# A pair that always runs is moved behind the branches of pairs, one key load to another queue, and the first expert output to another bank

## The chip, the cores and the metric

The kernel runs on one core of a Trainium2 chip. The metric is the device time of the execution in microseconds (us). The profile is one execution taken by the hardware profiler. Engines are named as it names them: PE is TensorE's matmuls, PEld its weight loads, DVE is VectorE, ACT ScalarE, POOL GpSimd, SP SyncE; a q behind a name (POOLq) is the engine's instruction queue.

## The reference

Sparse attention over 8 batches, 8 heads, 576 positions and 64 columns a head, half of the heads with a local mask and half with a strided one. Its output, 4608 rows of 512, goes into a mixture of 8 experts. Each row has one expert, chosen at run time:

```python
for s in range(S):
    fresh_e = int(np.argmax(logits[b, s]))
    if s == 0 or local_gate[b, s] < 0.5:
        e = fresh_e
    else:
        e = prev_e if prev_e >= 0 else fresh_e
    prev_e = e
    ...                                       # p: softmax of the logits
    h = np.maximum(x[b, s] @ w1[e], 0.0)      # 512 -> 1024
    out[b, s] = p[e] * (h @ w2[e])            # 1024 -> 512
```

Which rows an expert gets, and so how many tiles of 128 rows there are, is known only on the chip.

## The kernel before

Attention runs first and writes its rows to a buffer in DRAM (`xd`). Six expert tiles of early batches ("early" tiles) begin under its end. Then the router's counts are known, and the rest follows as a list of units `U`: *pairs* (two tiles of one expert, done with a Strassen-like scheme of seven products a layer), two *mixed* tiles (two halves of different experts) and *singles*. For a unit the kernel loads the expert's weights (`weights`, 4 MB in four pieces), gathers the rows (`gather`, an indirect DMA from GpSimd), turns them with transposes (`turn_x`, done one unit ahead, in the middle of the unit before), computes the hidden layer and the output, and scatters the result.

The numbers of the plan: eleven pairs are certain (`PAIR_MIN` is 11), up to sixteen may be needed (`PAIR_MAX`), and up to four singles.

```python
for k in range(PAIR_MIN):
    self.U.append(pair(k))
    ...                                        # a mixed tile after pairs 2 and 5
self.first = len(self.U)
self.U += [dict(rd=r2, ..., single=i) for i in range(SINGLES)]
self.last = len(self.U)
self.U += [pair(k) for k in range(PAIR_MIN, PAIR_MAX)]
for j, u in enumerate(self.U):
    u["set"] = j % 2 if j < self.last else 2 if j == self.last else (j - self.last - 1) % 2
...
for j, u in enumerate(self.U):
    ahead = self.first if j == self.last else j
    at = j - AHEAD if j < NE else self.first - 1 if j == self.last + 1 else ahead - 2
    self.gathers.setdefault(at, []).append(j)
    if j > 1:
        self.turns.setdefault(ahead - 1, []).append(j)
```

A unit turns the rows of the next one between its own hidden layer and its own output. For a pair, VectorE then builds the sums of rows (`xs`, four adds) and of weights (`t1`, four adds) that the seven products need:

```python
def unit(self, j, loads, nxt, step=lambda ins: None):
    ...
    self.hidden_pair(j)                 # sums of w2 (t2), then seven products
    ...
    for k in nxt:
        self.turn_x(k)
    self.output_pair(j)                 # seven products, two scatters
```

In the hidden layer the products of one bank form a chain, and ScalarE copies it out between them; VectorE's adds and ScalarE's relus stand in the same queues:

```python
product(chain, a11, b11, True);   nc.scalar.copy(out=p, in_=chain)
product(b7, s3, t3, True)
product(chain, s2, t2, False);    nc.scalar.copy(out=u, in_=chain)
product(b2, a12, b21, True);      row(b2, p, flat[0])     # row: VectorE add, ScalarE relu
nc.vector.tensor_tensor(u, b7, u, op=Alu.add)
product(chain, s1, t1, False);    nc.scalar.copy(out=v, in_=chain)
row(b7, v, flat[3])
product(b4, a22, t4, True);       row(b4, u, flat[2])
product(chain, s4, b22, False);   nc.scalar.activation(flat[1], chain, Act.Relu)
self.rows = self.sums_a(self.hs, hs)
```

The branches. All engines read the counts into registers and compare; where a branch is not taken, each engine jumps and adds to its semaphores what the branch would have added:

```python
for j in range(NE - 1, self.first):
    self.run(j)
singles, pairs = count(1, SINGLES), count(0, PAIR_MAX)
with ExitStack() as chain:
    for j in range(self.first, self.last):
        chain.enter_context(tc.If(singles > j - self.first))
        self.run(j)
for j in range(self.last, len(self.U)):
    ctx.enter_context(tc.If(pairs > self.U[j]["pair"]))      # closed at line 252
    self.run(j)
```

Behind all this the kernel asks whether the softmax without subtracted maximum was safe, and skips a careful second pass of everything if so:

```python
again = nc.values_load(bad[0:1, 0:1], ...)     # line 143
with tc.If(again > 0):                         # line 145
    ...
    passes(tc, True, ...)
```

Of the kernel before, what the change touches and what calls it, by code (L numbers as in the profile page):

```python
# [19 lines left out]
P = 128  # L20
# [251 lines left out]
def attention(ctx, tc, careful, psX, psS, fill, q, k, vl, vs, wg, xd, cc, codes, inv):  # L272
# [113 lines left out]
    def load_first():  # L386


        for n in range(2 * PAIRS + 2):
            if n == PAIRS + 2:  # L390
                nc.sync.dma_start(out=wgs[:, :, GC // 2:], in_=wg.rearrange("(k p) e -> p k e", p=P))
            if n < 2 * PAIRS:
                b, pair = divmod(n, PAIRS)
                grp, i2 = divmod(pair, 2)
                if i2 == 0:
                    places(b, grp)
                qt, kt = st["q", b, grp], st["k", b, grp]
                hq, hk = LT // 2 * LQ, LT // 2 * LQ + STRIDE
                for c, d in (((slice(0, hq), slice(0, hk)), (slice(hq, S), slice(hk, KW))) if n == 0 else
                             ((slice(0, S), slice(0, KW)),)):  # L400
                    nc.sync.dma_start(out=qt[:, i2, c], in_=q[b][:, pair, c])
                    (nc.sync if n else nc.scalar).dma_start(out=kt[:, i2, d], in_=k[b][:, pair, d])
            if n >= 2:
                b, pair = divmod(n - 2, PAIRS)
                grp, i2 = divmod(pair, 2)
                nc.sync.dma_start(out=st["v", b, grp][:, i2], in_=(vs if grp else vl)[b][:, i2])
# [478 lines left out]
class Experts:  # L885
# [14 lines left out]
    def __init__(self, ctx, tc, xd, w1, w2, views, c, r1, r2):  # L900
        self.tc, self.nc = tc, tc.nc
        self.xd, self.w1, self.w2, self.views, self.c = xd, w1, w2, views, c
        self.r1, self.r2 = r1, r2
        xp = ctx.enter_context(tc.tile_pool(name="xp", bufs=1))
        self.end = self.rows = None
        self.sets = [(xp.tile([P, DK, F], F32, name=f"w1t{i}"), xp.tile([P, FK, D], F32, name=f"w2t{i}"))
                     for i in range(1)]
        self.xg = Ring(xp, AHEAD + 1, [P, DX], "xg")
        self.xT = Ring(xp, 2, [P, D], "xgT")
        self.hT = Ring(xp, 2, [P, FK, P], "hT")  # L910
        self.pe = Ring(xp, 2, [P, 2, E], "pe")
        self.pt = Ring(xp, 2, [P, 2], "pt")
        self.pt2 = Ring(xp, 2, [P, 2], "pt2")

        self.U = [dict(rd=r1, at=i, cols=[i], rows=BE * S) for i in range(NE)]
        pair = lambda k: dict(rd=r2, at=k, cols=[2 * k, 2 * k + 1], rows=N, pair=k)
        for k in range(PAIR_MIN):
            self.U.append(pair(k))  # L920
            if k in MIXED:
                m = MIXED.index(k)
                self.U.append(dict(rd=r2, at=PAIR_MAX + SINGLES + m, cols=[2 * PAIR_MAX + SINGLES + m], rows=N,
                                   halves=[r2.units + 2 + 2 * m + h for h in range(2)]))
        self.first = len(self.U)
        self.U += [dict(rd=r2, at=PAIR_MAX + i, cols=[2 * PAIR_MAX + i], rows=N, single=i) for i in range(SINGLES)]
        self.last = len(self.U)
        self.U += [pair(k) for k in range(PAIR_MIN, PAIR_MAX)]
        for j, u in enumerate(self.U):
            u["set"] = j % 2 if j < self.last else 2 if j == self.last else (j - self.last - 1) % 2  # L930
        ones = [u for u in self.U if "pair" not in u]
        for i, u in enumerate(ones):
            u["xg"], u["xT"], u["hT"] = self.xg[i], self.xT[i], self.hT[i]

        self.gathers, self.turns, self.extra = {}, {}, {}
        for j, u in enumerate(self.U):
            ahead = self.first if j == self.last else j
            at = j - AHEAD if j < NE else self.first - 1 if j == self.last + 1 else ahead - 2  # L940
            self.gathers.setdefault(at, []).append(j)
            if j > 1:
                self.turns.setdefault(ahead - 1, []).append(j)
            if "halves" in u or j == self.last:
                w = self.weights(j, int(j != self.last))
                self.extra[ahead - 3], self.extra[ahead - 2] = w[:2], w[2:]

    def later(self, ctx):

        self.banks = Banks(ctx.enter_context(self.tc.tile_pool(name="pse", bufs=1, space=PSUM)))  # L950
        self.banks.ring.used = 3
# [24 lines left out]

    def gather(self, j):
        u = self.U[j]
        if "pair" in u:
            u["xg"] = self.xg2.next()  # L980
        for a, i in enumerate(u["cols"]):
            self.nc.gpsimd.indirect_dma_start(  # L982
                out=u["xg"][:, a] if "pair" in u else u["xg"], out_offset=None, in_=self.xd[0:u["rows"]],
                in_offset=bass.IndirectOffsetOnAxis(ap=u["rd"].gi[:, i:i + 1], axis=0))

    def turn_x(self, j):

        nc, u = self.nc, self.U[j]
        n = len(u["cols"])
        x = u["xg"] if "pair" in u else u["xg"].rearrange("p (a d) -> p a d", a=1)  # L990
        to = self.xT2 if "pair" in u else u["xT"].rearrange("p (a d) -> p a d", a=1)
        for a in range(n):
            ps = self.bank()
            for kk in range(DK):
                self.product(nc.tensor.transpose, ps[:, kk * P:(kk + 1) * P], x[:, a, kk * P:(kk + 1) * P],
                             self.c.ident)
            if "pair" in u:
                nc.scalar.copy(out=to[:, a], in_=ps)
            else:
                ins = nc.vector.tensor_copy(to[:, a], ps).ins  # L1000

        pe, u["pt"] = self.pe.next(), (self.pt2 if "pair" in u else self.pt).next()
        with self.tc.issue_after(ins if n == 1 else self.rows) if n == 1 or self.rows else nullcontext():
            nc.vector.tensor_tensor(pe[:, 0:n], x[:, :, D:DX], across(u["rd"].oh[:, u["at"]], [P, n, E]), op=Alu.mult)
            self.turned = nc.vector.tensor_reduce(u["pt"][:, 0:n], pe[:, 0:n], axis=AX.X, op=Alu.add).ins
            if "pair" in u:
                self.sums_a(self.xs, self.blocks_x())
                self.sums_b(self.t1, self.blocks_w(self.sets[u["set"]][0]))

    def sums_a(self, s, blocks):  # L1010
        v, (a11, a12, a21, a22) = self.nc.vector, blocks
        v.tensor_tensor(s[:, 0], a21, a22, op=Alu.add)
        v.tensor_tensor(s[:, 1], s[:, 0], a11, op=Alu.subtract)
        v.tensor_tensor(s[:, 2], a11, a21, op=Alu.subtract)
        return v.tensor_tensor(s[:, 3], a12, s[:, 1], op=Alu.subtract).ins

    def sums_b(self, t, blocks):

        v, (b11, b12, b21, b22) = self.nc.vector, blocks
        v.tensor_tensor(t[:, 0], b12, b11, op=Alu.subtract)  # L1020
        v.tensor_tensor(b12, b22, b12, op=Alu.subtract)  # L1021
        v.tensor_tensor(t[:, 1], b22, t[:, 0], op=Alu.subtract)
        v.tensor_tensor(t[:, 2], b21, t[:, 1], op=Alu.subtract)  # L1023

    def blocks_x(self):
        x = self.xT2.rearrange("p a (k m) -> p a k m", k=DK)
        return [x[:, a, k:k + DK // 2] for a in range(2) for k in (0, DK // 2)]

    def blocks_w(self, w):
        k, f = w.shape[1] // 2, w.shape[2] // 2  # L1030
# [10 lines left out]

    def hidden_pair(self, j):
        nc = self.nc
        w1, w2 = self.sets[self.U[j]["set"]]
        self.sums_b(self.t2, self.blocks_w(w2))
        a11, a12, a21, a22 = self.blocks_x()
        b11, t3, b21, b22 = self.blocks_w(w1)
        s1, s2, s3, s4 = (self.xs[:, i] for i in range(4))
        t1, t2, t4 = (self.t1[:, i] for i in range(3))
# [29 lines left out]
        row(b4, u, flat[2])  # L1079
        product(chain, s4, b22, False)  # L1080
        nc.scalar.activation(flat[1], chain, Act.Relu)
        self.rows = self.sums_a(self.hs, hs)

    def output_pair(self, j):

# [40 lines left out]

    def hidden_mixed(self, j):

        nc, xT = self.nc, self.U[j]["xT"]
        for f in range(2):  # L1130
            ps = self.bank()
            for kk in range(DK):
# [20 lines left out]
    def hidden_blocks(self, j, pool=None):  # L1153

        nc, u = self.nc, self.U[j]
        w1, xT, hT = self.sets[u["set"]][0], u["xT"], u["hT"]
# [68 lines left out]
    def run(self, j, step=lambda ins: None):  # L1225
# [2 lines left out]
            self.gather(k)  # L1228


        if self.last <= j < len(self.U) - 1:
            for piece in self.weights(j + 1):
                piece()
        loads = self.weights(j + 2) if j + 2 < self.last else []
        for i, piece in enumerate(self.extra.get(j, [])):
# [21 lines left out]
    def rest(self, ctx):  # L1257
# [77 lines left out]
```

## Time and profile before

| | |
|---|---|
| device time, median of 3 | 679.09 us (678.66 to 679.68) |
| span of the profiled execution | 674.9 us |
| mean granted TensorE clock | 0.988 of full speed |
| HBM read, written | 159.80 MB, 19.55 MB |
| last matmul ends | 656.4 us |

The span runs from the first to the last instruction of the profile and lies a few us under the device time. A slice of the page is a fortieth of the span, 16.9 us. Where a helper records all operations (line 1039 for the products, line 371 for VectorE in attention), operations are told apart by their tiles. The profiler counts branches, semaphores, register loads and drains as not busy; the view of a single line shows them with their times.

### The profile page before, as it was taken

The page shows a single profiled execution, that of the slowest core. Times are in us where ns is not written, and L with a number is a line of the kernel's source. Part 1 is how long each engine was busy: PE and PEld are TensorE (multiplying, and loading weights), DVE is VectorE, ACT ScalarE, POOL GpSimd, SP SyncE. Part 2 cuts the span into 40 slices and gives each one's busy share as a digit, 9 for nine tenths or more (in the row PEclk, how much of TensorE's full clock was granted, in tenths as well). Part 3 has the DMA queues.
Part 4 walks back from the last instruction along what each step waited for, and adds up shares of the span by engine and source line. Part 5 has one row for each costly group of instructions (what it writes and reads, how often), then busy time and mean ns, then how long its engine had stood idle before and what let it go on. Part 6 is the DMA issues. An engine that isn't in the chain of part 4 may idle for free.

```text
span 674.9 us, 14639 instructions
## 1 busy us (share of the span) xinstructions
PE 652.1 (97%) x5926; PEld 554.1 (82%) x5926; DVE 392.7 (58%) x805; ACT 188.7 (28%) x390; POOL 156.3 (23%) x200
## 2 busy tenths in 40 slices
PE   9999999999999999999999999999999999999990
PEld 8898888777767799996699984999999996869970
DVE  8686889634561556856295673569569530205660
ACT  4555545421111231322123221322322311113220
POOL 2444444540034311201121102112112011011210
PEclk9999999999999999999999999999999999999995
DMA  9999999559989988776868858675687758577200
GB/s 327 400 408 411 329 326 337 152 157 401 401 290 295 389 303 307 267 281 209 299 223 300 301 189 290 212 241 165 240 300 257 281 178 333 200 268 294 65 18 21
DMA packets 70849, 179.94 MB, mean 267 GB/s; under 512 B 12110, under 2 KB 12622, under 8 KB 70768
## 3 DMA queue, kind: packets, MB, share of 16 engines
q1 hardware_dynamic: 58704, 148.47, 61.1%
q0 software_dynamic: 11776, 30.08, 13.5%
q8 instruction: 51, 0.84, 0.5%
q10 hardware_dynamic: 288, 0.31, 0.1%
q14 instruction: 30, 0.25, 0.1%
HBM read 159.80 MB, written 19.55 MB: 266 GB/s over the span
## 4 chain that ended last, share of the span: by engine, by line
PE 90%; DVE 4%; DMA 2%; issue 1%; ACT 0%; POOL 0%; DVEq 0%; POOLq 0%; ACTq 0%
PE bank L1039 49%; PE bank L1188 10%; PE bank L1162 10%; PE vps L366 6%; PE xps L366 5%; PE sps L366 5%; PE bank L1184 2%; DMA w2t<-in_w_dram 2%; PE sps L1162 1%; DVE e L371 1%; DVE xl L371 0%; DVE lane L841 0%; DVE xs L371 0%; DVE t L1023 0%; DVE w2t L1021 0%
## 5 line engine op out<-in xcount | busy, mean ns | idle before, releaser
L1198 POOL DMA_INDIRECT out_dram<-y,si x38 | 49.4, 1300 | 278.0 <-DVE y L1107 147.0
L982 POOL DMA_INDIRECT xg<-xd,gi x42 | 47.5, 1131 | 146.3 <-PE bank L1039 128.6
L1188 PE MATMUL bank<-w2t,hT 128*128 128x512 f32 x160 | 70.9, 594 | 0.8 <-ACT hT L1165 0.8
L1162 PEld LDWEIGHTS bank<-xgT,w1t 128*128 128x128 f32 x576 | 65.4, 192 | 2.0 <-issue 1.7
L1162 PE MATMUL bank<-xgT,w1t 128*128 128x128 f32 x576 | 66.2, 276 | 0.0
L1188 PEld LDWEIGHTS bank<-w2t,hT 128*128 128x128 f32 x160 | 29.5, 190 | 34.5 <-issue 32.5
L495 POOL DMA_DIRECT2D xd<-xs x80 | 44.9, 567 | 48.1 <-DVE gsm L575 17.3
L1074 DVE TENSOR_TENSOR part<-bank,part 128x512 f32<-128x512 f32 x13 | 9.0, 692 | 78.8 <-ACT part L1071 78.8
L1039 PEld LDWEIGHTS bank<-xT,w1t 128*128 128x128 f32 x416 | 49.5, 192 | 3.1 <-issue 2.6
L1039 PE MATMUL bank<-xT,w1t 128*128 128x128 f32 x416 | 51.3, 276 | 0.0
L1039 PE MATMUL bank<-xs,w1t 128*128 128x128 f32 x416 | 50.7, 275 | 0.0
L1039 PE MATMUL bank<-xs,t 128*128 128x128 f32 x416 | 50.7, 275 | 0.0
L1039 PE MATMUL bank<-w2t,h 128*128 128x256 f32 x208 | 49.2, 379 | 0.0
L1039 PE MATMUL bank<-w2t,hs 128*128 128x256 f32 x208 | 49.1, 379 | 0.0
L1039 PE MATMUL bank<-t,hs 128*128 128x256 f32 x208 | 49.1, 379 | 0.0
L1039 PEld LDWEIGHTS bank<-xs,w1t 128*128 128x128 f32 x416 | 48.5, 192 | 0.0
L1039 PEld LDWEIGHTS bank<-xs,t 128*128 128x128 f32 x416 | 48.5, 192 | 0.0
L1064 DVE TENSOR_TENSOR h<-bank,part 128x512 f32<-128x512 f32 x39 | 27.0, 692 | 34.7 <-ACT part L1076 22.9
L366 PE MATMUL sps<-qt,kt 64*128 64x96 f32 (+2 forms) x704 | 46.3, 277 | 0.2
L366 PEld LDWEIGHTS sps<-qt,kt 64*128 64x128 f32 (+2 forms) x704 | 40.6, 184 | 5.1 <-issue 2.6
L423 ACT ACTIVATE e<-sps 128x576 f32<-128x576 f32 (+1 forms) x64 | 39.9, 649 | 15.7 <-PE sps L366 12.4
L1104 ACT ACTIVATE part<-bank,pt 128x256 f32<-128x256 f32 x39 | 18.5, 474 | 92.0 <-PE bank L1039 92.0
(271 smaller groups left out, 1039.7 us busy)
## 6 DMA issues: line engine op xcount, KB each, us to landing
w1t<-in_w_dram SPq DMA_DIRECT2D x56, 1024.0 KB
w2t<-in_w_dram SPq DMA_DIRECT2D x56, 1024.0 KB
kt<-in_k_dram SPq DMA_DIRECT2D x12, 608.0 KB
qt<-in_q_dram SPq DMA_DIRECT2D x12, 576.0 KB
vlt<-in_vl_dram SPq DMA_DIRECT2D x6, 780.0 KB
xd<-xl POOLq DMA_DIRECT2D x16, 288.0 KB
vst<-in_vs_dram SPq DMA_DIRECT2D x6, 650.0 KB
xd<-xs POOLq DMA_DIRECT2D x48, 54.0 KB
```

The costliest lines, as they stand in the source:

```text
L366: st["pe"] = product(*args, **kw).ins
L423: nc.scalar.activation(ev, ps[0:kb, :, 0:m * w], Act.Exp, bias=0.0, scale=1.0 / DH ** 0.5)
L495: nc.gpsimd.dma_start(out=dst[h, :, c:c + n], in_=src[h * HALF:h * HALF + n * SP // 2, t])
L982: self.nc.gpsimd.indirect_dma_start(out=u["xg"][:, a] if "pair" in u else u["xg"], out_offset=None, in_=self.xd[0:u["rows"]], in_offset=ba ...
L1039: self.end = fn(*args, **kw).ins
L1064: nc.vector.tensor_tensor(to, ps, add, op=Alu.add)
L1074: nc.vector.tensor_tensor(u, b7, u, op=Alu.add)
L1104: nc.scalar.activation(to, ps, Act.Copy, scale=g[r])
L1162: ins = nc.tensor.matmul(ps[:, i * P:(i + 1) * P], lhsT=w1[:, kk, c], rhs=xT[:, kk * P:(kk + 1) * P], start=(kk == 0), stop=(kk == DK - 1))
L1184: ins = nc.tensor.matmul(ps[s], lhsT=hT[:, kk, s], rhs=w[:, kk, :], start=(kk == 0), stop=(kk == FK - 1))
L1188: ins = nc.tensor.matmul(ps, lhsT=hT[:, kk], rhs=w2[:, kk, :], start=(kk == 0), stop=(kk == FK - 1))
L1198: self.nc.gpsimd.indirect_dma_start(out=self.views[0], in_=y, in_offset=None, bounds_check=N - 1, oob_is_err=False, out_offset=bass.Indire ...
```

## The change

It has three parts, and some rewriting that they need.

*The order of the pairs.* Pairs 9 and 10, both certain, leave the place ahead of the singles. Pair 9 stands directly behind the singles, without a branch. Pairs 11 to 15 follow in their nested branches. Pair 10 comes last, behind all branches. The aim is that the work which skipping a branch needs lies ahead of a pair's arithmetic and not at the end of the program. Since the pair before the last one is not known until run time, the last pair's rows are gathered and turned in pair 9 already, its weights are loaded there into the third buffer set, and its turned rows and sums lie in tiles of the singles that are free by then (`xg`, `xT`, `hT`, `y`, `h`).

*Keys of the second pair of heads.* Their load is issued from ScalarE's queue, no longer from SyncE's behind the others.

*The first output's bank.* The ring of eight PSUM banks starts at 6, not at 3.

The rewriting: rows and sums are lists of views in place of one tile, and the product of gate weights with the one-hot choice is one VectorE instruction a tile, not one a pair.

```diff
@@ load_first
-                    (nc.sync if n else nc.scalar).dma_start(out=kt[:, i2, d], in_=k[b][:, pair, d])
+                    (nc.sync if n > 1 else nc.scalar).dma_start(out=kt[:, i2, d], in_=k[b][:, pair, d])
@@ the list of units
-        for k in range(PAIR_MIN):
+        for k in range(PAIR_MIN - 2):
...
-        self.U += [pair(k) for k in range(PAIR_MIN, PAIR_MAX)]
+        self.U += [pair(k) for k in (PAIR_MIN - 2, *range(PAIR_MIN, PAIR_MAX), PAIR_MIN - 1)]
+        self.end_j = len(self.U) - 1
         for j, u in enumerate(self.U):
-            u["set"] = j % 2 if j < self.last else 2 if j == self.last else (j - self.last - 1) % 2
+            u["set"] = j % 2 if j < self.last else 1 if j == self.end_j else (2, 0)[(j - self.last) % 2]
...
-            ahead = self.first if j == self.last else j
-            at = j - AHEAD if j < NE else self.first - 1 if j == self.last + 1 else ahead - 2
+            ahead = self.first if j == self.last else self.last + 1 if j == self.end_j else j
+            at = self.last if j == self.end_j else j - AHEAD if j < NE else self.first - 1 if j == self.last + 1 else ahead - 2
@@ later
-        self.banks.ring.used = 3
+        self.banks.ring.used = 6
@@ gather
+        if j == self.end_j:
+            u["xg"] = [self.xg[a] for a in range(2)]
+            u["xT"] = [self.xT[a] for a in range(2)]
+            u["xs"] = [self.y[i // 2].rearrange("p (i k m) -> p i k m", i=2, m=P)[:, i % 2] for i in range(4)]
+            u["t1"] = [t.rearrange("p (k f) -> p k f", k=DK // 2) for t in
+                       [self.hT[i].rearrange("p k m -> p (k m)") for i in range(2)] + [self.h]]
@@ turn_x
-            nc.vector.tensor_tensor(pe[:, 0:n], x[:, :, D:DX], across(u["rd"].oh[:, u["at"]], [P, n, E]), op=Alu.mult)
+            for a in range(n):
+                nc.vector.tensor_tensor(pe[:, a], x[a][:, D:DX], u["rd"].oh[:, u["at"]], op=Alu.mult)
@@ run
-        if self.last <= j < len(self.U) - 1:
-            for piece in self.weights(j + 1):
+        if self.last <= j < self.end_j - 1:
+            pieces = self.weights(j + 1)
+            if j == self.last:
+                w = self.weights(self.end_j)
+                pieces = pieces[:2] + w[:2] + pieces[2:] + w[2:]
+            for piece in pieces:
                 piece()
@@ rest
-        for j in range(self.last, len(self.U)):
-            ctx.enter_context(tc.If(pairs > self.U[j]["pair"]))
-            self.run(j)
+        self.run(self.last)
+        with ExitStack() as chain:
+            for j in range(self.last + 1, self.end_j):
+                chain.enter_context(tc.If(pairs > self.U[j]["pair"]))
+                self.run(j)
+        self.run(self.end_j)
```

More of the change, by code (lines that the diff above doesn't have):

```diff
@@ L978, in gather @@
         u = self.U[j]
-        if "pair" in u:
-            u["xg"] = self.xg2.next()
+        if j == self.end_j:
[4 more added lines that the diff above has]
+                       [self.hT[i].rearrange("p k m -> p (k m)") for i in range(2)] + [self.h]]
+        elif "pair" in u:
+            x = self.xg2.next()
+            u["xg"], u["xT"] = [x[:, a] for a in range(2)], [self.xT2[:, a] for a in range(2)]
+        else:
+            u["xg"], u["xT"] = [u["xg"]], [u["xT"]]
         for a, i in enumerate(u["cols"]):
             self.nc.gpsimd.indirect_dma_start(
-                out=u["xg"][:, a] if "pair" in u else u["xg"], out_offset=None, in_=self.xd[0:u["rows"]],
+                out=u["xg"][a], out_offset=None, in_=self.xd[0:u["rows"]],
                 in_offset=bass.IndirectOffsetOnAxis(ap=u["rd"].gi[:, i:i + 1], axis=0))
@@ L988, in turn_x @@
         nc, u = self.nc, self.U[j]
-        n = len(u["cols"])
-        x = u["xg"] if "pair" in u else u["xg"].rearrange("p (a d) -> p a d", a=1)
-        to = self.xT2 if "pair" in u else u["xT"].rearrange("p (a d) -> p a d", a=1)
+        n, x, to = len(u["cols"]), u["xg"], u["xT"]
         for a in range(n):
@@ L994, in turn_x @@
             for kk in range(DK):
-                self.product(nc.tensor.transpose, ps[:, kk * P:(kk + 1) * P], x[:, a, kk * P:(kk + 1) * P],
+                self.product(nc.tensor.transpose, ps[:, kk * P:(kk + 1) * P], x[a][:, kk * P:(kk + 1) * P],
                              self.c.ident)
             if "pair" in u:
-                nc.scalar.copy(out=to[:, a], in_=ps)
+                nc.scalar.copy(out=to[a], in_=ps)
             else:
-                ins = nc.vector.tensor_copy(to[:, a], ps).ins
@@ L1002, in turn_x @@
-        pe, u["pt"] = self.pe.next(), (self.pt2 if "pair" in u else self.pt).next()
+                ins = nc.vector.tensor_copy(to[a], ps).ins
+        pe, u["pt"] = self.pe.next(), (self.pt2 if "pair" in u and j != self.end_j else self.pt).next()
         with self.tc.issue_after(ins if n == 1 else self.rows) if n == 1 or self.rows else nullcontext():
-            nc.vector.tensor_tensor(pe[:, 0:n], x[:, :, D:DX], across(u["rd"].oh[:, u["at"]], [P, n, E]), op=Alu.mult)
+            for a in range(n):
+                nc.vector.tensor_tensor(pe[:, a], x[a][:, D:DX], u["rd"].oh[:, u["at"]], op=Alu.mult)
@@ L1005, in turn_x @@
             self.turned = nc.vector.tensor_reduce(u["pt"][:, 0:n], pe[:, 0:n], axis=AX.X, op=Alu.add).ins
             if "pair" in u:
-                self.sums_a(self.xs, self.blocks_x())
-                self.sums_b(self.t1, self.blocks_w(self.sets[u["set"]][0]))
+                if j != self.end_j:
+                    u["xs"], u["t1"] = [self.xs[:, i] for i in range(4)], [self.t1[:, i] for i in range(3)]
+                self.sums_a(u["xs"], self.blocks_x(u))
+                self.sums_b(u["t1"], self.blocks_w(self.sets[u["set"]][0]))
@@ L1010, in sums_a @@
     def sums_a(self, s, blocks):
         v, (a11, a12, a21, a22) = self.nc.vector, blocks
[L1012 to L1015, printed above, removed]
+        v.tensor_tensor(s[0], a21, a22, op=Alu.add)
+        v.tensor_tensor(s[1], s[0], a11, op=Alu.subtract)
+        v.tensor_tensor(s[2], a11, a21, op=Alu.subtract)
@@ L1017, in sums_b @@
+        return v.tensor_tensor(s[3], a12, s[1], op=Alu.subtract).ins
     def sums_b(self, t, blocks):
         v, (b11, b12, b21, b22) = self.nc.vector, blocks
-        v.tensor_tensor(t[:, 0], b12, b11, op=Alu.subtract)
+        v.tensor_tensor(t[0], b12, b11, op=Alu.subtract)
         v.tensor_tensor(b12, b22, b12, op=Alu.subtract)
[L1022 to L1027, printed above, removed]
+        v.tensor_tensor(t[1], b22, t[0], op=Alu.subtract)
@@ L1029, in blocks_w, with blocks_x @@
+        v.tensor_tensor(t[2], b21, t[1], op=Alu.subtract)
+    def blocks_x(self, u):
+        x = [t.rearrange("p (k m) -> p k m", k=DK) for t in u["xT"]]
+        return [x[a][:, k:k + DK // 2] for a in range(2) for k in (0, DK // 2)]
     def blocks_w(self, w):
@@ L1043, in hidden_pair @@
         nc = self.nc
-        w1, w2 = self.sets[self.U[j]["set"]]
-        self.sums_b(self.t2, self.blocks_w(w2))
-        a11, a12, a21, a22 = self.blocks_x()
+        u = self.U[j]
+        w1, w2 = self.sets[u["set"]]
+        self.sums_b([self.t2[:, i] for i in range(3)], self.blocks_w(w2))
+        a11, a12, a21, a22 = self.blocks_x(u)
         b11, t3, b21, b22 = self.blocks_w(w1)
-        s1, s2, s3, s4 = (self.xs[:, i] for i in range(4))
-        t1, t2, t4 = (self.t1[:, i] for i in range(3))
+        (s1, s2, s3, s4), (t1, t2, t4) = u["xs"], u["t1"]
         h11, h12, h21, h22 = hs = [self.h2[:, i] for i in range(4)]
@@ L1081, in hidden_pair @@
         nc.scalar.activation(flat[1], chain, Act.Relu)
-        self.rows = self.sums_a(self.hs, hs)
+        self.rows = self.sums_a([self.hs[:, i] for i in range(4)], hs)
     def output_pair(self, j):
@@ L1127, in hidden_mixed @@
     def hidden_mixed(self, j):
-        nc, xT = self.nc, self.U[j]["xT"]
+        nc, xT = self.nc, self.U[j]["xT"][0]
         for f in range(2):
@@ L1155, in hidden_blocks @@
         nc, u = self.nc, self.U[j]
-        w1, xT, hT = self.sets[u["set"]][0], u["xT"], u["hT"]
+        w1, xT, hT = self.sets[u["set"]][0], u["xT"][0], u["hT"]
         for g in range(FK // self.HB):
```

## The prediction

> **What bounds the kernel now.** I read first the page's busy shares and slices, then the end of the timeline, then the views of single lines that hold branches, semaphores and register loads, which the page leaves out of its busy time. First the page of the kernel before, shares and slices:
>
> ```profile
> PE 652.1 (97%) x5926; PEld 554.1 (82%) x5926; DVE 392.7 (58%) x805; ACT 188.7 (28%) x390; POOL 156.3 (23%) x200
> ...
> PE   9999999999999999999999999999999999999990
> DMA  9999999559989988776868858675687758577200
> ```
>
> TensorE is busy in every slice but the last, and DMA is saturated only in the first seven. So a change pays only if it takes TensorE work away, closes a TensorE gap, or shortens that last slice. I listed every gap of over 0.15 us between matmul records: they sum to 4.0 us, 1.5 of it ahead of the first matmul. The rest of what is not TensorE is the tail. The timeline of the end (start, duration, engine, line; two stretches of one view):
>
> ```profile
> 643.26 1.04 PE L1039 MATMUL bank<-ident,xg 128*128 128x128 f32 x8
> 643.52 0.60 ACT L1081 ACTIVATE h<-bank 128x512 f32<-128x512 f32 x1 [0.49 <-PE bank L1039]
> ...
> 644.13 1.89 PE L1039 MATMUL bank<-w2t,h 128*128 128x256 f32 x8
> ...
> 656.47 0.47 ACT L1104 ACTIVATE y<-bank,pt 128x256 f32<-128x256 f32 x1 [2.97 <-PE bank L1039]
> 657.22 1.01 POOL L1198 DMA_INDIRECT out_dram<-y,si  x1 [1.91 <-ACTq L252]
> ```
>
> The last matmul ends at 656.38, the last scatter starts at 657.22, and the span is 674.88: 17.66 us follow the last scatter with no arithmetic in them. What they are, by lines: L252 closes the branches of pairs, L143 and L145 ask whether the careful second pass is needed, L1331 ends the program (columns: engine's queue, operation, count, shortest/median/longest ns, first and last start). Of L252:
>
> ```profile
> L252 PEldq COMPARE_BRANCH  x4: 71/125/3709, 598.2 to 657.6; - x4
> ...
> L252 POOLq EVENT_SEMAPHORE  x4: 17/43/3462, 657.2 to 660.8; - x4
> ...
> L252 ACTq EVENT_SEMAPHORE  x1: 17/17/17, 657.0 to 657.0; - x1
> L252 PEldq EVENT_SEMAPHORE  x1: 51/51/51, 657.3 to 657.3; - x1
> L252 POOLq INC_SWDGE_SEM  x1: 1646/1646/1646, 660.9 to 660.9; - x1
> ```
>
> Of L143, then L145, then L1331:
>
> ```profile
> L143 POOLq TENSOR_LOAD <-bad x1: 300/300/300, 662.8 to 662.8; - x1
> ```
>
> ```profile
> L145 POOLq EVENT_SEMAPHORE  x6: 17/30/43, 665.8 to 666.3; - x6
> ...
> L145 POOLq COMPARE_BRANCH  x1: 50/50/50, 663.1 to 663.1; - x1
> L145 POOLq INC_SWDGE_SEM  x1: 1628/1628/1628, 666.3 to 666.3; - x1
> ```
>
> ```profile
> L1331 POOLq DRAIN  x3: 46/107/6032, 668.0 to 674.6; - x3
> ```
>
> The reader sees GpSimd alone carrying the tail, one step after another: it waits 3.46 us for the last scatter to land (657.23 to 660.69), makes up the counts of the branches not taken (1.65), loads the flag, jumps (663.1 to 665.8, 2.7 us until its next instruction), makes up the counts of the pass not taken (1.63), drains (6.03), and closes (0.85). The other engines are through with theirs by 663.
>
> **What the Trainium skill says.** Runtime: NRT & Kernel Launch, section Instruction fetch mechanics: a taken branch to a target outside the loaded pages waits for a fetch. The trace agrees: of TensorE's four L252 branches the one that jumps takes 3709 ns, the shortest 71. DMA: Bandwidth & Descriptors, Anatomy of one DMA — SWDGE (gpsimd) path: a transfer's semaphore fires only when the write is confirmed, about 2 us of fixed cost; the scatter here takes 3.46, which I use. The same page, Issuing engines are not separate DMA queues: another issuing queue saves issue time, not bandwidth; no run here shows it yet. Advanced Engine Details and Errata, Engine Queue Depths: TensorE's queue holds many instructions. The trace agrees: that branch was issued at 653.57, 2.8 us before the last matmul ended.
>
> **The change part by part.** Thirteen pairs ran (L1074 x13) and all four singles (L1188 x160 is ten outputs of 16 records, six of them early). So pairs 11 and 12 are taken, 13 is not. Before, the untaken branch comes after all work. After, the order is pairs 0 to 8, singles, 9, 11, 12, the untaken branch, and pair 10 last.
>
> 1. *Tail.* The L252 bookkeeping (landing wait, 1.65 us of counts, branch) moves to the join ahead of pair 10, where GpSimd has some 20 us until it is needed. Behind the last scatter remain the flag, the jump, one count, the drain. Flag and jump take 0.4 + 2.7 = 3.1 us and now run while the scatter lands (3.5 us). New tail from the scatter: 3.5 landing + 0.25 semaphores + 1.65 count + 6.05 drain + 0.85 close = 12.3 us, against 17.66. Gain 5.4 us. I choose to keep the drain at 6.03, which I cannot explain.
>
> 2. *The join on TensorE.* The same untaken branch now stands between two pairs. By the trace TensorE's jump ends at 657.28, its semaphore follows at 657.34, a short branch at 657.56 (0.18), and the next instruction issues at 657.80. With a weight load, the next product starts near 658.0, where the last one ended at 656.38. In the built program that first product of pair 10 also waits for counts of ScalarE and VectorE that only their own untaken sides add, but those come at 657.0 and 655.3, earlier. Cost 1.6 us.
>
> 3. *Eight transposes.* Pair 10's gathered rows are now turned in pair 9, beside pair 11's: TensorE does 16 instead of 8 there. One group takes from 643.26 to 644.13, 0.87 us of the path. In the last pair they are missing, but their place is exactly the wait for ScalarE's last relu (643.52 + 0.60 = 644.12, and the output product starts at 644.13), so nothing comes back. Cost 0.9 us. The useless turn and load of pair 13 exist in both.
>
> 4. *VectorE in pair 9.* One turn's sums take 6.2 us (645.67 to 651.91). A second set now follows ahead of the output rows. The rows then end about 29.6 us after the pair's first product instead of 24.4; the pair is 25.5 + 0.9 long, so 3.2 us into pair 11; the w2 sums (4.9 us) and the branch then reach to 8.6. Two adds of 0.69, a relu of 0.63 and a copy of 0.59, one after another across two engines, end at 11.2, and the product that waits for the copy is due at 10.8. Cost 0.4 us, taken as 0.3.
>
> 5. *Weights.* Pair 9 now issues 8 MB. Before, pair 11 did the same for 12 and 13 one branch later. The first loads go at 593, when the last single's hidden products end; at the 350 to 370 GB/s of the windows from 600 to 620 all are in by 616, while the second w1 is needed at 626. Cost 0.
>
> 6. *Bank.* The first output product starts behind a gap of 0.83 us; timeline:
>
> ```profile
> 147.02 0.69 DVE L1000 COPY xgT<-xps 128x512 f32<-128x512 f32 x1 [0.48 <-PE xps L1039]
> ...
> 147.81 1.96 PE L1188 MATMUL bank<-w2t,hT 128*128 128x512 f32 x4 [0.83 <-ACT hT L1165]
> ```
>
> It starts as that VectorE copy ends (147.71). In the built program it waits for the same counts, VectorE 341 and ScalarE 184, with either bank; only the bank's name differs. Gain 0.
>
> 7. *Keys.* The second pair's keys leave about 0.5 us sooner. But the second pair's scores started at 7.70 behind ScalarE's exponent (0.25 us idle, released by it), with their loads in. Gain 0, either sign 0.3.
>
> 8. *Small products.* One more VectorE instruction of about 0.1 us per pair, in slack. Cost 0.
>
> Sum: -5.4 + 1.6 + 0.9 + 0.3 = -2.6 us. From the median of 679.1: 676.5 us.
>
> **Rivals.** *The join eats the gain.* If the jump is not hidden by matmuls in flight, or the code of pair 10 must be fetched again after it, the gap is 3.7 to 5 us. For it: the jump is the longest branch of the kernel. Against: half of it lay behind queued matmuls. Time then: 678.5 to 680. *The drain swells.* If the 6.03 us wait for something that is tied to the last scatter, a shorter way there is partly given back; time 678 to 679. Or it shrinks with one count instead of two behind the scatter; 672 to 674. *The second weight load or the sums stall TensorE in pair 11 or 12.* Only two buffers alternate now, the third is held for pair 10. For it: w1 of pair 12 cannot be loaded before pair 9's hidden products end. Against: that leaves 29 us for a 2 MB load of 6. Time if wrong: 679 to 682. *The bank or the keys pay after all*: another 0.5 to 1 us, 675.5.
>
> **Range and chances.** The terms of the sum are each good to about 1 us and the repeats before span 1.0 us, so 674.3 to 678.9 should hold the time 8 times in 10. A change of 2% is 13.6 us, more than any tail step here; 0.01 faster, 0.98 same, 0.01 slower.
>
> **What would show it.** Right: the span ends about 12.3 us after the last scatter, with one INC_SWDGE_SEM there and the other more than 15 us earlier; a TensorE gap of 1.3 to 2 us ahead of the last pair; 16 transposes in one run in the first pair after the singles; the first output still starting as the VectorE copy ends, near 147.8. Wrong: a gap at the join over 3 us, a drain far from 6 us, a gap in pair 11 over 1 us, or a first output near 147.

## The result, and the profile after

The changed kernel takes 673.5 us (median of 4, 673.15 to 674.47), the kernel before in the same comparison 678.88 us (median of 4, 676.80 to 679.68): ratio 0.9928, 95% interval 0.9903 to 0.9953. So 4.9 us less by the ratio, 5.4 by the medians, where 2.6 was predicted. The profiled spans, 674.9 and 671.1 us, differ by 3.8. Lines shift: what was 1039 (products) is 1053, 1198 (scatter) is 1212, 252 (branches of pairs) is 1301, 1331 (end) is 1352; 143 and 145 stay.

The page of the changed kernel, shares and slices:

```profile
PE 651.5 (97%) x5926; PEld 553.3 (82%) x5926; DVE 393.2 (59%) x819; ACT 189.1 (28%) x390; POOL 183.0 (27%) x200
...
PE   9999999999999999999999999999999999999992
DMA  9999999559989988785958858687868669655001
```

TensorE does the same work, and of its slices only the last moves, from 0 to 2. First the start of pair 12, then the timeline of the changed kernel from the join on, the join being the place of the untaken branch between pair 12 and the last pair (start, duration, engine, line; two stretches of one view):

```profile
605.86 1.95 PE L1053 MATMUL bank<-xT,w1t 128*128 128x128 f32 x16
```

```profile
632.85 2.02 PE L1053 MATMUL bank<-xgT,w1t 128*128 128x128 f32 x16 [1.36 <-PEq L1301]
...
645.43 1.89 PE L1053 MATMUL bank<-w2t,h 128*128 128x256 f32 x8
645.69 0.60 ACT L1095 ACTIVATE h<-bank 128x512 f32<-128x512 f32 x1 [0.49 <-PE bank L1053]
...
657.77 0.47 ACT L1118 ACTIVATE y<-bank,pt 128x256 f32<-128x256 f32 x1 [2.97 <-PE bank L1053]
658.52 0.98 POOL L1212 DMA_INDIRECT out_dram<-y,si  x1 [1.94 <-ACT y L1118]
```

The gap at the join is 1.36 us. What the join costs is a little more, because in an unbroken run of products the record of one overlaps the start of the next by 0.16 us (the one ahead of pair 12 runs from 604.13 for 1.89). From the first product of pair 12 to the first of the last pair there are 26.99 us (605.86 to 632.85), where other pairs with eight transposes take 25.47, and the last pair's first product takes 2.02 us, not 1.95. That makes 1.6 us. The last matmul ends at 657.68, 1.3 us later than before, and yet the span ends 3.8 us earlier. The branches of pairs (line 1301; count, shortest/median/longest ns, first and last start) now lie ahead of that pair:

```profile
L1301 PEldq COMPARE_BRANCH  x4: 71/130/3607, 578.2 to 632.5; - x4
...
L1301 POOLq EVENT_SEMAPHORE  x4: 17/43/3097, 632.3 to 632.5; - x4
...
L1301 POOLq INC_SWDGE_SEM  x1: 1610/1610/1610, 635.7 to 635.7; - x1
```

What is left behind the last scatter, by the lines 145 and 1352:

```profile
L145 POOLq EVENT_SEMAPHORE  x6: 17/30/601, 661.4 to 662.5; - x6
...
L145 POOLq COMPARE_BRANCH  x1: 50/50/50, 658.7 to 658.7; - x1
L145 POOLq INC_SWDGE_SEM  x1: 1627/1627/1627, 662.5 to 662.5; - x1
```

```profile
L1352 POOLq DRAIN  x3: 46/107/6032, 664.2 to 670.8; - x3
```

GpSimd's branch is at 658.7 and its next instruction at 661.4: the jump runs while the scatter lands, and only 0.60 us of the landing remains to be waited for. Then come one count, the same drain, and the end, 12.6 us behind the scatter's start in place of 17.7.

### The profile page after: what moved, and what is told of

Its sections match the earlier page's. It is cut to its first block, busy times and chain, and to the rows that moved or that the text cites. A ratio compares the mean times of both kernels' runs of the same rounds, so it can differ in the third digit from the quotient of the medians.

```text
span 671.1 us, 14648 instructions
## 1 busy us (share of the span) xinstructions
PE 651.5 (97%) x5926; PEld 553.3 (82%) x5926; DVE 393.2 (59%) x819; ACT 189.1 (28%) x390; POOL 183.0 (27%) x200
## 5 line engine op out<-in xcount | busy, mean ns | idle before, releaser
L995 POOL DMA_INDIRECT xg<-xd,gi x42 | 73.5, 1750 | 132.5 <-DVE xs L1026 95.5
L1053 PEld LDWEIGHTS bank<-xT,w1t 128*128 128x128 f32 x384 | 45.7, 192 | 3.1 <-issue 2.6
L1053 PE MATMUL bank<-xT,w1t 128*128 128x128 f32 x384 | 47.4, 276 | 0.0
L1053 PE MATMUL bank<-xs,w1t 128*128 128x128 f32 x384 | 46.8, 275 | 0.0
L1053 PE MATMUL bank<-xs,t 128*128 128x128 f32 x384 | 46.8, 275 | 0.0
L1053 PEld LDWEIGHTS bank<-xs,w1t 128*128 128x128 f32 x384 | 44.8, 192 | 0.0
L1053 PEld LDWEIGHTS bank<-xs,t 128*128 128x128 f32 x384 | 44.8, 192 | 0.0
```

Of the source, the lines that this page charges most:

```text
L995: self.nc.gpsimd.indirect_dma_start(out=u["xg"][a], out_offset=None, in_=self.xd[0:u["rows"]], in_offset=bass.IndirectOffsetOnAxis(ap=u["r ...
L1053: self.end = fn(*args, **kw).ins
```

## The experiments

The first four ask which part of the change pays, and what the kernel before does from one execution to the next.

**Keys alone.**

```diff
-                    (nc.sync if n else nc.scalar).dma_start(out=kt[:, i2, d], in_=k[b][:, pair, d])
+                    (nc.sync if n > 1 else nc.scalar).dma_start(out=kt[:, i2, d], in_=k[b][:, pair, d])
```

> The kernel before with the keys' part alone. Theory A (the 0.55 us that TensorE was ahead at 7 us came from the clock: matmuls of the first scores took 272 ns each instead of 418, with no wait between them): the keys gain nothing, ratio 0.999 to 1.001, time 678 to 679; the second pair's scores start at 7.2 to 7.7, at either end by chance. Rival (the keys' own gain): 0.5 us, ratio 0.9992, and the second pair's scores start by 7.2 in every execution. The two differ by less than the repeats may resolve; the profile's first matmuls decide.

677.98 us, ratio 0.9999 (0.9991 to 1.0008). The reason for asking: TensorE stood 0.55 us ahead at 7 us in the changed kernel's profile. Here, with the keys on the new queue, it stood behind. The tile of scores between 5.4 and 7.1 us, in the kernel before, the changed kernel, this one, and the kernel before in another execution (the control below):

```profile
L366 PE MATMUL sps<-qt,kt x18: 271/272/526, 5.6 to 7.0; 64*128 64x96 f32 x18
```

```profile
L366 PE MATMUL sps<-qt,kt x24: 272/272/347, 5.5 to 6.8; 64*128 64x96 f32 x24
```

```profile
L366 PE MATMUL sps<-qt,kt x14: 381/417/526, 5.6 to 7.0; 64*128 64x96 f32 x14
```

```profile
L366 PE MATMUL sps<-qt,kt x28: 272/272/347, 5.2 to 7.1; 64*128 64x96 f32 x28
```

The same matmul takes 272 or 417 to 526 ns, and the moment at which the fast rate begins differs between executions of one kernel. The second pair's scores start at 7.70, 7.15, 7.97 and 6.87 us: each 0.05 to 0.06 us behind ScalarE's exponent of the first pair's scores, and so by the rate of the first matmuls, not by the keys. No gain of the keys shows; the interval alone would still hold one of 0.6 us. That the rate is the clock's, as theory A has it, is not shown: the granted clock reads 1.00 in either case.

**Order alone**: the changed kernel with keys and bank put back (`n > 1` to `n`, 6 to 3).

> The changed kernel with keys and bank put back: the order of the pairs alone. Theory A (all of the gain is the order's): tail from last scatter 12.5 us, join gap 1.36, span 671 to 672, time within 0.5 us of the changed kernel's 673.5, so 673 to 674; ratio 0.992 to 0.994. Rival (keys and bank pay 0.5 to 1 us): 674.0 to 674.5.

674.4 us (median of 6), ratio 0.9944 (0.9929 to 0.9959); join gap 1.25 us, 13.0 us from the last scatter to the end. The median lies in the rival's range (674.0 to 674.5), and the interval of the ratio holds both theories. What speaks for theory A are the runs of the keys alone and of the bank alone, which show no gain. The span of 672.9 lies 1.8 us above that of the changed kernel: 0.46 us of it stand ahead of the first output, 0.45 behind the last scatter, and the remaining 0.9 between 216 and 415 us, outside the parts changed.

**Bank alone**: `ring.used` 3 to 6.

> The kernel before with the first output's bank alone. Theory: no gain, the first output still starts as VectorE's copy of the gathered rows ends, with a gap of 0.83 us near 147.8; ratio 0.999 to 1.001. Rival (the bank held it): gap under 0.4 us and 0.4 to 0.5 us less time.

678.38 us, ratio 1.0008 (0.9995 to 1.0021). The first output starts at 147.28 behind a gap of 0.83, as in every kernel here. The rival's 0.4 to 0.5 us less is excluded.

**The kernel before once more.**

> The kernel before once more, unchanged, to see what its repeats do. The profiled execution had a span of 674.9 us and 676.6 us device time, while three others took 678.7 to 679.7. Theory A (the first profile was a quick execution, and the usual one is some 2 us longer): most spans here are 676 to 678, and the extra 2 us can be found at some place in a profile that falls among them. Rival (the spans are alike and only time outside the span differs): spans of 674.5 to 675.5 with device times of 678 to 679.7.

678.01 us (median of 14), ratio 1.0000 (0.9992 to 1.0008), spans 675.1 to 677.3; the 43 executions beside it have spans of 673.8 to 678.3 and 1.7 to 1.9 us outside the span. So the rival falls, spans scatter by over 4 us, and the first profile, at 674.9, lies at their lower end. This profile, at 675.1, is a quick one too, so it can't show where the usual execution loses its time. Two places show across the profiles: in those of the old order the first output starts between 146.95 and 148.75 us, and the landing of the last scatter varies. GpSimd's wait for it, which begins with the scatter, lasts 3.46, 3.73, 3.82, 4.72 and 4.92 us in five profiles of the old order (the kernel before, this one, keys alone, bank alone, no turn for pair 13), and 3.35 in a sixth (no flag in the kernel before).

**No flag in the changed kernel**: the question for the second pass and that pass are left out.

```diff
-    again = nc.values_load(bad[0:1, 0:1], ...)
-    with tc.If(again > 0):
-        ...
-        passes(tc, True, ...)
```

> The changed kernel without the question for the second pass and without the second pass, which is left out altogether (these data do not need it). Theory A (flag and jump lie under the landing of the last scatter): only the count of 1.63 us and the semaphores go, so the tail from the last scatter is 10.6 to 10.9 us in place of 12.55, time 1.6 to 1.9 us less, near 672. Rival (the drain of 6.03 us waits for the scatter's writes): the drain grows by what is removed, tail 12.0 to 12.6, no gain. Second rival (program size sets the jumps): the join's jump of 3.6 us shrinks with half of the program gone, and the join's gap falls below 1 us.

670.67 us, ratio 0.9884 (0.9867 to 0.9901): some 3 us less than the changed kernel in the other comparisons. Theory A had sized it at 1.6 to 1.9, and its tail at 10.6 us or more; the tail is 7.9 us, 4.7 less. The time falls by less than the tail, as the last matmul of this profile ends 2.8 us later than that of the changed kernel's first one: 0.7 us later at the first output, and 2.1 more at waits between 302 and 416 us. Why is not shown. The timeline of the end and the view of the closing line:

```profile
661.27 0.98 POOL L1203 DMA_INDIRECT out_dram<-y,si  x1 [1.94 <-ACT y L1109]
```

```profile
L1343 POOLq DRAIN  x3: 51/112/7256, 661.0 to 668.9; - x3
```

The drain starts ahead of the scatter's record and ends at 668.29, 6.04 us after the end of that record. It takes its 6.03 us from GpSimd's own last work; no wait for the landing stands ahead of it, and with the 3.35 to 4.92 us seen elsewhere the landing fits under it. So neither rival holds: the drain took up nothing that was removed, and the join's jump is 3589 ns and its gap 1.35 us with half of the program gone. What theory A missed is that the count waits for the landing, and not the end of the program: without the count, the wait goes too.

**No flag in the kernel before**: the same edit.

> The kernel before with the same left out. Theory A (there flag, jump and count follow each other behind the untaken branch of pairs): 0.4 + 2.7 + 1.65 and semaphores go, 4.8 to 5.0 us; tail 12.7 to 13.0 us in place of 17.66, time 673 to 673.5. This is three times what the same edit gives in the changed kernel. Rival (the drain takes up what is removed): tail 16 us or more, gain under 2 us.

671.86 us, ratio 0.9913 (0.9893 to 0.9932). The tail from the last scatter is 12.3 us in place of 17.7. Here the landing is still waited for, since the count of the untaken pairs stands behind the scatter:

```profile
L243 POOLq EVENT_SEMAPHORE  x4: 17/43/3347, 657.6 to 661.1; - x4
...
L243 POOLq INC_SWDGE_SEM  x1: 1646/1646/1646, 661.2 to 661.2; - x1
```

The edit takes 5.4 us off this tail and 4.7 off that of the changed kernel, not three times as much: in the changed kernel it removes a jump that runs beside the landing, but also the last wait for it. Theory A had 4.8 to 5.0 us for this tail and a time of 673 to 673.5; in the kernel before, 5.37 us lay between the last branch of pairs and the drain (662.63 to 668.00), here 0.12. The rival falls.

**No turn for pair 13, in the kernel before.** Its rows are turned at the start of pair 13 and not in pair 12. These data never reach pair 13, so its eight transposes are left out.

```diff
-            if j > 1:
+            if j > 1 and j != 25:
                 self.turns.setdefault(ahead - 1, []).append(j)
...
+        if j == 25:
+            self.end = self.rows = None
+            self.turn_x(j)
         self.unit(j, loads, self.turns.get(j, []), step)
```

> The kernel before, where pair 13's rows are turned at the start of pair 13 itself and no longer in pair 12. Pair 13 is not reached with these data, so its eight transposes are left out. Theory A (transposes ahead of the output cost their full 0.87 us, also in a last pair): the last pair lasts 24.8 us from its first product to its last, not 25.6; the last matmul ends near 655.5 and the time falls by 0.9, to 677.2; the first output product starts as the last hidden one ends, some 0.5 us ahead of the end of the last relu. Rival (the prediction's: the place is the wait for the last relu): the first output product still starts with the end of the last relu, a gap of some 0.5 to 0.9 us stands ahead of it, and nothing is gained.

677.24 us, ratio 0.9991 (0.9980 to 1.0002), which alone doesn't tell. The timeline does; its end:

```profile
641.24 1.95 PE L1039 MATMUL bank<-xs,w1t 128*128 128x128 f32 x16
...
643.03 1.25 PE L1039 MATMUL bank<-w2t,h 128*128 128x256 f32 x5
643.29 0.60 ACT L1081 ACTIVATE h<-bank 128x512 f32<-128x512 f32 x1 [0.49 <-PE bank L1039]
```

The output begins 1.79 us after the last hidden product began, which is one product's time, and 0.26 us before the last relu even starts. The place was no wait for the relu. The last pair lasts 24.76 us from its first matmul to its last, where it was 25.63: the transposes cost their 0.87 us.

**The same edit in the changed kernel** (`j == 24`).

> The changed kernel with the same edit: pair 13's rows are turned at the start of pair 13, which is not reached. Theory A: pair 12 is 0.87 us shorter, so the span falls by 0.9 from what the changed kernel has, time 672.6 to 673.2 where the changed kernel's usual time is 673.5 to 674.1; ratio 0.991 to 0.993. Rival (the place is the wait for the relu): no change, and a gap ahead of pair 12's first output product. If VectorE was near its limit in pair 12, the join could shrink too; by theory A it stays at 1.25 to 1.4 us.

673.92 us, ratio 0.9936 (0.9918 to 0.9955), not told from the changed kernel's 0.9934 below. In the timeline pair 12's first output product follows its last hidden one by 1.79 us (617.14 to 618.93), where the changed kernel has 2.66 (616.58 to 619.24): 0.87 us gone. In the span most of it is hidden: ahead of pair 12 this profile stands 0.56 us behind the changed kernel's first one, 0.24 at the first output and the rest at waits near 320 and 413 us. The join's gap is 1.33.

The last four were run beside the changed kernel itself, all against the same executions of the kernel before (676.19 us in the median there, 22 executions).

**The changed kernel once more.**

> The changed kernel once more, unchanged, beside many executions of the kernel before. Theory A (the real gain is what the spans show, some 4 us, and the 5.4 us of the first comparison had three slow executions of the kernel before in it): time 673.5 to 674.5, 3.8 to 4.5 us under the kernel before, ratio 0.9935 to 0.9945. Rival (the first comparison was right): 5 us or more, ratio under 0.9926.

671.96 us (median of 9), ratio 0.9934 (0.9910 to 0.9958), 4.5 us by the ratio. Nearer theory A; the interval (2.8 to 6.1 us) doesn't exclude the rival. The absolute time is 1.5 us under what was expected, and the kernel before is 1.9 to 2.7 us lower in this comparison than in the others. Its join gap is 1.10 us, its branch 3347 ns.

**No skipped branch**: pairs 13 to 15 are left out of the program.

```diff
-        self.U += [pair(k) for k in (PAIR_MIN - 2, *range(PAIR_MIN, PAIR_MAX), PAIR_MIN - 1)]
+        self.U += [pair(k) for k in (PAIR_MIN - 2, *range(PAIR_MIN, 13), PAIR_MIN - 1)]
```

> The changed kernel with pairs 13 to 15 left out of the program, so that no branch of pairs is skipped with these data: no jump on any engine ahead of the last pair, and no turn for pair 13. Theory A (the join's gap on TensorE is its jump): the gap ahead of the last pair falls from 1.36 us to under 0.2, pair 12 is 0.87 us shorter, 2.1 us less in all, span 668.5 to 669.5, time 671.4 to 672.2. Rival (the gap is a wait for VectorE, ScalarE or GpSimd, or a cold weight load): a gap of 0.8 us or more stays, time 672.7 to 673.3.

669.32 us, ratio 0.9901 (0.9868 to 0.9934), 2.6 us under the changed kernel beside it (the absolute time expected was worked out from an earlier, higher comparison). TensorE's branches and the timeline at the join:

```profile
L1301 PEldq COMPARE_BRANCH  x3: 71/71/173, 576.9 to 626.5; - x3
```

```profile
627.66 1.67 PE L1053 MATMUL bank<-w2t,hs 128*128 128x256 f32 x7
629.17 1.95 PE L1053 MATMUL bank<-xgT,w1t 128*128 128x128 f32 x16
```

No gap: the join's cost is the skipped branch. From the first product of pair 12 to the first of the last pair there are 24.59 us (604.58 to 629.17), in the changed kernel beside it 26.73 (605.12 to 631.85). Of these 2.14 us 0.87 are the turn's and 1.27 the join's, where the gap shows 1.10. The edit takes the jump from every engine at once. In the changed kernel ScalarE adds its counts of the untaken side at 632.1 us and TensorE is through with its jump at 632.3; in the profile beside this one both come at 631.3. Whether TensorE would wait for ScalarE if its own jump were shorter was not tried.

**A shorter skip**: pairs 14 and 15 left out, so that the jump passes one pair and not three (`range(PAIR_MIN, 14)`).

> The changed kernel with only pairs 14 and 15 left out, so that the skipped branch holds one pair and not three. Theory A (a jump over code costs a fixed fetch): TensorE's longest branch stays at 3.5 to 3.7 us, the gap at 1.25 to 1.45, time as the changed kernel. Rival (the jump costs by the code that it skips): 1.2 to 2 us for the branch, the gap under 0.3 us, 1.1 us less.

671.45 us, ratio 0.9930 (0.9908 to 0.9952). TensorE's branch and the gap:

```profile
L1301 PEldq COMPARE_BRANCH  x4: 71/130/3347, 576.2 to 630.2; - x4
```

```profile
630.58 2.02 PE L1053 MATMUL bank<-xgT,w1t 128*128 128x128 f32 x16 [1.10 <-PEq L1301]
```

The same 3347 ns and 1.10 us as the whole changed kernel beside it (both under the range expected, from an earlier comparison). Over one pair or three, the jump doesn't cost by what it skips.

**The last scatter behind the flag.** If the count is what waits for the landing, the count can stand ahead of the last scatter. Its rows are kept in a tile that outlives the first pass (`ylast`), and its row numbers are raised by 4608 for every bad partition, so that after a second pass it would write nothing.

```diff
     with tc.If(again > 0):
         ...
         passes(tc, True, ...)
+    nc.gpsimd.indirect_dma_start(out=last["view"], in_=ylast, in_offset=None, bounds_check=N - 1, oob_is_err=False,
+                                 out_offset=bass.IndirectOffsetOnAxis(ap=last["si"][:, 0:1], axis=0))
...
+            self.nc.vector.tensor_tensor(last["si"], last["f"], last["off"], op=Alu.add)
```

> The changed kernel with the last scatter moved behind the question for the second pass (its row numbers are pushed out of bounds where the second pass is to run, so that it then writes nothing). Theory A (what follows the last work of GpSimd is only its drain of 6.03 us, and a landing lies under the drain): flag, jump, landing of the other scatter and the count now lie ahead of the last scatter, which starts at 3 to 3.8 us behind the last matmul in place of 0.84; the span ends 7.9 us behind its start; 1.4 to 2.2 us less than the changed kernel, 671.5 to 672.5. Rival (the drain waits for the landing when nothing else did): the drain grows to 8.5 us or more and nothing is gained.

670.42 us (median of 6), ratio 0.9910 (0.9876 to 0.9944): 1.5 us under the changed kernel beside it. The intervals of the two ratios overlap; five of its six spans (667.9 to 668.9, the sixth 670.5) lie under all nine of the changed kernel (669.3 to 671.2). The end of its timeline, and its closing line:

```profile
656.24 0.47 ACT L1126 ACTIVATE inv<-bank,pt 128x256 f32<-128x256 f32 x1 [2.92 <-PE bank L1059]
661.07 0.98 POOL L155 DMA_INDIRECT out_dram<-inv,silast  x1 [5.97 <-issue]
```

```profile
L1368 POOLq DRAIN  x3: 46/112/7249, 660.8 to 668.7; - x3
```

The span ends 7.9 us after the start of the last scatter, as expected, and the drain again ends 6.04 us after the scatter's record; the rival falls. The scatter starts 4.9 us behind the last matmul, later than the 3 to 3.8 expected: the other scatter must still land and be counted first (until 659.83), and a further 1.2 us pass to the start of this one. Of the kernels that leave out nothing, this has the lowest median.

## Why the prediction was wrong in size

The mechanism was right, and the time fell below the range. By its own steps, with the two first profiles, and with the mean of five profiles of each order (old order: the five of the landings above; changed order: the changed kernel twice, order alone, no turn, shorter skip, the last with a drain 0.16 us shorter):

| step | predicted | first two profiles | means |
|---|---|---|---|
| 1 tail from the last scatter | -5.4 | 17.66 to 12.57: -5.1 | 18.31 to 12.71: -5.6 |
| 2 join | +1.6 | +1.6 | +1.5 |
| 3 eight transposes | +0.9 | 0 | 0 |
| 4 VectorE in pair 11 | +0.3 | 0 | 0 |
| 5 to 8 | 0 | 0 | 0 |
| sum of the steps | -2.6 | -3.5 | -4.1 |
| start and waits outside the change | | -0.3 | -0.8 |
| span | | -3.8 | -4.9 |

The last two rows of the means are no gain of the change, since the profiles come from several comparisons, in one of which the kernel before is quicker too.

1. *Tail*: right. Flag and jump went under the landing, and the drain stayed at 6032 ns. The landing stands in both tails and so drops out of the gain, but for its scatter: it took 3.46 us in the first profile of the kernel before and 3.80 in that of the changed kernel (658.52 to 662.32), and this is the 0.3 us by which the first two profiles miss the 5.4.

2. *Join*: the mechanism was right, and the size came out partly by luck. The prediction worked out a gap of 1.6 us; the gap is 1.36, and 1.10 to 1.38 in other profiles. The overlap that is lost (0.16) and the slower first product (0.07), which it did not have, make 1.6 of it in the first profile and 1.3 to 1.6 in the others. The experiment without a skipped branch has no gap at all. The rival that pair 10's code must be fetched after the jump falls. (The jump is not the longest branch of the kernel, as the prediction has it for this rival: TensorE's branch of line 145 takes 4147 ns in the same profile.)

3. *Eight transposes*: this is the step that failed. "Their place is exactly the wait for ScalarE's last relu, so nothing comes back" took two ends that fell together, 644.12 and 644.13, for a wait. The code says what the product reads:

```python
product(chain, a11, b11, True)       # output_pair: the first product reads h[0]
...
nc.scalar.activation(flat[1], chain, Act.Relu)   # hidden_pair: the last relu writes h[1]
```

In the changed kernel the output product of the last pair (645.43) starts ahead of that relu (645.69). The added transposes cost 0.87 us in pair 9, and their absence gave it back in the last pair. Pair 9, timeline:

```profile
564.77 1.95 PE L1053 MATMUL bank<-xs,w1t 128*128 128x128 f32 x16
566.56 1.91 PE L1053 MATMUL bank<-ident,xg 128*128 128x128 f32 x16
568.30 1.89 PE L1053 MATMUL bank<-w2t,h 128*128 128x256 f32 x8
```

Pair 9 is 26.34 us long (554.05 to 580.39) and pair 11, with eight transposes, 25.47; the last pair is 24.83 (632.85 to 657.68) where it was 25.63 before. The work was moved, not added; the experiment in the kernel before shows the same 0.87 without any reordering.

4. *VectorE*: the backlog is there, but smaller. Pair 11 starts at 580.39; its product that waits for the last copy, timeline:

```profile
586.44 1.27 DVE L1037 TENSOR_TENSOR t<-w2t,t 128x1024 f32<-128x1024 f32 x1
...
589.58 0.59 ACT L1090 COPY part<-bank 128x512 f32<-128x512 f32 x1
...
591.11 1.95 PE L1053 MATMUL bank<-xs,w1t 128*128 128x128 f32 x16
```

The output rows of pair 9 end 2.45 us into pair 11, not 3.2, and the sums follow without the half microsecond that the prediction had between. So the sums end 7.3 us into the pair, not 8.6, and the copy 9.8, not 11.2; the product was placed right, at 10.7 (10.8 predicted), and 0.9 us of slack remain.

5. to 8. Right: no gap over 0.15 us in pairs 11 and 12, the first output starts as the VectorE copy ends (gap 0.83 with either bank), keys and bank alone pay nothing.

Steps 3 and 4 are 1.2 us. Without them the prediction's own sum is -3.8 us. The first comparison has 4.9 us by the ratio (3.2 to 6.6), the second 4.5 (2.8 to 6.1), and order alone 3.8 (2.8 to 4.8), so 3.8 lies within all three intervals. The rest of the first comparison's 4.9, or 5.4 by the medians, can't be told from the scatter of the executions, and no run assigns it to a step. That the span of the first two profiles also differs by 3.8 is in part luck: the tail is 0.3 us short of its 5.4 there, and the start and the waits outside the change give 0.3 us back.

## What to carry to other kernels

Bookkeeping of a skipped branch belongs where its engine has time, and each wait in it should be asked what it waits for: here the count of the untaken side waited for a transfer that the end of the program would have covered. Two events that end together in a trace are no dependence; look up which tile the later one reads before work between them is called free. For a change of under 1%, take the terms from several executions: the landing alone varied from 3.35 to 4.92 us.

## What was not expected of the hardware

- The drain at the end ends 6.03 to 6.04 us after GpSimd's last work, whether or not the scatter had been seen to land before it: 6032 ns behind a count, 7256 and 7249 ns where it includes a scatter's issue. With fewer pairs in the program it was 5869 (one skipped) and 5706 ns (none). What it does in that time, and why it shrinks, is open.
- TensorE's jump takes 3347 ns over one pair or three, and 3589 ns in half the program. Between executions of the changed order it varied from 3.35 to 3.63 us. TensorE reaches it while matmuls are still in flight, so that a jump of 3.35 us shows as a gap of 1.10.
- The first matmuls ran at 417 to 526 ns or at 272 ns, while the view of time windows gives a granted clock of 1.00 for 5.5 to 6.5 us in either case. What sets the moment of change wasn't tried.
